# A tile's five loads each placed by its own priority on SyncE's queue, six buffers for a and v, and a new set of priorities

## The chip, the core and the metric

The kernel runs on one core of a Trainium2 chip. The metric is the device time of one execution in microseconds (us). Five engines work side by side, each through its own instructions in a fixed order: PE (matmuls and transposes on the tensor array; its weight loads are shown as PEld), DVE, ACT and POOL (elementwise work), and SP, which only issues DMA transfers. They wait for each other through semaphores.

## What is computed

A recurrent attention (RWKV-7) over 4 batches, 8 heads, 768 steps and head size 40, and then a mixer over the tokens.

```
for t in range(S):
    y[t]  = r[t] @ state
    Sa    = state @ a[t]
    state = state * w[t] - outer(Sa, b[t]) + outer(v[t], k[t])

x = y as (batch, token, 320)
theta = x @ w_theta
y2 = w_tok_r @ (x * cos(theta)) + w_tok_i @ (x * sin(theta))
u = x + y2
out = u + max(u @ w_ch, 0)
```

The time loop isn't run step by step. It is cut into chunks of 128 steps, and within a chunk it becomes matrix products.

## The kernel before

A **tile** is one chunk of 128 steps of one batch with all heads; there are 6 tiles in a batch and 24 in all, numbered 0 to 23. Each tile goes through these stages.

1. Loads (`loads`, line 414): six arrays of 160 KB in float32, `w`, `k`, `b`, `a`, `v` by SP, one transfer each, and `r` for two tiles at a time in two transfers. The tiles that take them in, `raw_w`, `raw_kb`, `raw_a`, `raw_v`, are rings of four buffers, so a load of tile i waits until tile i-4 has read its buffer.
2. `prep` (line 435): ACT takes the logarithm of `w` (`lw`, L441), PE sums it over time (`cs`, L448 to L456), ACT takes the exponential (`ex`, L460). With it `k` and `b` (`kb`, L468) and `a` (`ah`, L472) are scaled, on POOL, for the first two tiles on DVE. `v` and `r` are only cast (L477, L497). PE transposes them (L398, L505), and ACT brings the results out of PSUM (`kbT`, `aT`, `vT`, `rT`; L401, L509).
3. Scores (line 515): PE multiplies 64-row halves (L522), and DVE masks the products (L527), giving `psi`, `phi`, `lamv` and, later, `lamu`. One mask takes about 1.2 us.
4. `recurrence` (line 542): the chain from tile to tile. `x0` on PE (L555, L561) needs `psi`; ACT copies it (`nx`, L567); `nu` on PE (L573) needs `phi`; ACT copies it (L577). Then the new state `gt` (L586, L591) goes through DVE (L599), and the next tile's `x0` needs it.
5. `readout` (line 631): `lamu`, then `y` (L652, L654), and DVE writes `x` (L661). A transpose (L625) and `theta` (L670) follow.
6. The mixer, once a batch's tiles are there: sines and cosines on ACT (L690, L694), for which ACT needs another table of functions (a table load), products `zr`, `zi` on POOL (L706), rows (`row`, L724), `u` on DVE (L734), its transpose, the product with `w_ch` (L670), the sum on DVE (L743), and a store by SP (L746). The token weights are loaded by POOL (L764), transposed by PE (L772) and copied by DVE (L776).

**What sets the order.** None of these instructions is issued where it stands in the code. `add` only notes each with its engine, a cost in ns, and what it reads and writes. When all steps (their numbers run to 1456) are noted, `Plan.order` (line 95) plays the whole program through with these costs: each time it takes, for each engine, the steps that are ready, gives each a score, its priority plus `WAIT` times how much later it could start than the first that could, takes the lowest, and goes on. ACT pays `TSWITCH` in its score for a change of table. The order so found is then the order in which each engine is given its instructions. The priority is

```
o.prio = 1000.0 * (TIMES[o.spec[0]][o.spec[1]] + OFF[o.spec[2]])
```

that is, a time for the tile (or row, or weight block) plus an offset for the kind of the step. All five loads of a tile are of the kind `load`, so they have the same priority and stay in the order `w, k, b, a, v`. The numbers in `TIMES` and `OFF` were found by a search. PSUM's banks are also handed out by this play (`find`): two pairs for scores and `cs`, four single ones for the rest. Data are never read before they are there, whatever the order: each wait is a semaphore. A bad order only makes an engine wait at one instruction while others behind it could run.

Of the kernel before, what the change touches and what calls it, by code (L numbers as in the profile page):

```python
# [9 lines left out]
FP32 = mybir.dt.float32  # L10
BF16 = mybir.dt.bfloat16
AF = mybir.ActivationFunctionType
ALU = mybir.AluOpType
# [20 lines left out]
class Plan:  # L34
# [34 lines left out]
    def link(self):  # L69
        ops = self.ops  # L70
        users = {}
        for o in ops:
            o.succ = []
            o.npre = len(o.pre)
            o.start = o.end = None
            o.banks = None
            o.prio = 1000.0 * (TIMES[o.spec[0]][o.spec[1]] + OFF[o.spec[2]])
            for k in set(o.reads) | set(o.writes):
                if k[0] == "ps":
                    users.setdefault(k, set()).add(o)  # L80
        for o in ops:
            o.soft = set()
            if o.new is not None and not o.loose:
                u = users[o.new[0]]
                o.soft = {p for x in u if x is not o for p in x.pre if p not in u}
                o.soft -= set(o.pre)
            o.npre += len(o.soft)
        for o in ops:
            for p in o.pre:
                p.succ.append(o)  # L90
            for p in o.soft:
                p.succ.append(o)
        return users

    def order(self):
# [44 lines left out]
        while len(out) < n:  # L140
            pick = None
            for e, lst in ready.items():
                if not lst:
                    continue
                te = free[e]
                if e == "SP":
                    te = max(te, dma - SP_DEPTH)
                cand = []
                lo = None
                for o in lst:  # L150
                    t = max(te, est0[o])
                    b = None
                    if o.new is not None:
                        f = find(o)
                        if f is None:
                            continue
                        t = max(t, f[0])
                        b = f[1]
                    if e == "PE" and o.mode != mode:
                        t = max(t, te + (INTO64 if o.mode == 64 else OUTOF64))  # L160
                    cand.append((t, o, b))
                    if lo is None or t < lo:
                        lo = t
                if lo is None:
                    continue
                best = None
                for t, o, b in cand:
                    s = o.prio + WAIT * (t - lo)
                    if e == "ACT" and o.table is not None and o.table != table:
                        s += TSWITCH  # L170
                    if best is None or (s, o.idx) < best[0]:
                        best = ((s, o.idx), t, o, b)
                if pick is None or best[1] < pick[1]:
                    pick = best
            if pick is None:
                raise RuntimeError("no bank: " + str({e: [(o.kind, o.i) for o in l] for e, l in ready.items()}))
            _, t, o, b = pick
            ready[o.eng].remove(o)
            if o.eng == "ACT" and o.table is not None and o.table != table:
                table = o.table  # L180
                t += 1283
            o.start = t
            if o.new is not None:
                o.banks = b
                home[o.new[0]] = b
                for x in b:
                    bank_held[x] = True
            if o.eng == "PE":
                mode = o.mode
                o.end = t + o.cost + o.tail  # L190
                free["PE"] = t + o.cost
            elif o.work:
                free[o.eng] = t + o.cost
                if o.eng == "SP":
                    dma = max(dma, t + 1350.0) + o.work
                    o.end = dma + 600.0
                else:
                    s = max(t + 1800.0, dma - SP_DEPTH)
                    dma = max(dma, s) + o.work
                    o.end = min(dma, s + 2.0 * o.work) + 1000.0  # L200
            else:
                o.end = t + o.cost
                free[o.eng] = o.end - OVERLAP[o.eng]
            for k in set(o.reads) | set(o.writes):
                if k[0] == "ps":
                    left[k] -= 1
                    last_use[k] = max(last_use.get(k, 0.0), o.end + 50)
                    if left[k] == 0:
                        for x in home[k]:
                            bank_held[x] = False  # L210
                            bank_free[x] = last_use[k]
            out.append(o)
            for x in o.succ:
                x.npre -= 1
                if x.npre == 0:
                    make_ready(x)
# [10 lines left out]
def tail(n):  # L227
# [1 line left out]


OFF = dict(
    ah=-14.03, ch=37.4, cs=-41.22, ea=-6.95, egd=-90.74, egt=-28.2, ekb=21.31, enu=-16.72,
    enut=-11.56, er=-13.46, eth=-25.65, eut=-58.98, ev=17.32, ewt=-9.73, ex=39.26, exp=-63.71,
    ext=-55.21, gd=7.06, gt=16.39, kb=36.69, ln=-32.13, load=-20.04, loadr=-19.62, mlu=62.71,
    mlv=10.93, mphi=44.82, mpsi=69.12, nu=-17.14, nut=12.45, nx=-78.15, oo=13.49, r=35,
    row=38.73, sin=86.83, slu=-15.77, slv=39.92, sphi=-32.67, spsi=-35.87, st=34.23, ta=1.11,
    th=36.56, tkb=-1, tr=0.69, tv=4.86, uadd=-6.95, ut=37.54, v=-26.35, wdma=123.77, wt=37.8,
    x0=-27.08, xt=21.68, y=-40.12, z=24.68)
WAIT, TSWITCH = 435.08, 606442.0
TIMES = dict(  # L240
    tile=[
        -61.22, -38.55, -36.31, -3.78, 3.05, 10.64, 15.26, 42.47, 45.62, 46.74, 54.55, 58.02,
        77.61, 85.12, 102.64, 108.62, 104.48, 129.91, 135.62, 135.6, 150.73, 158.77, 165.34,
        174.78],
    row=[
        47.97, 37.38, 30.67, 33.44, 59.07, 74.74, 77.47, 97.12, 115.85, 115.75, 105.42, 129.53,
        141.42, 164.22, 173.87, 137.03, 124.06, 133.88, 191.51, 200.6, 184.9, 268.51, 279.77,
        212.96],
    rel=[
        -48.76, 34.55, 63.09, 65.85, -76.89, 92.41, 33.44, 33.52])  # L250


@with_exitstack
def kernel(
# [30 lines left out]
        return [consts.tile(shape, dt, name=f"{name}_{i}") for i in range(n)]  # L285

    raw_w = sb("raw_w", [128, H, D], FP32, 4)
    raw_a = sb("raw_a", [128, H, D], FP32, 4)
    raw_kb = sb("raw_kb", [128, 2, H, D], FP32, 4)
    raw_v = sb("raw_v", [128, H, D], FP32, 4)  # L290
    raw_r = sb("raw_r", [128, 2, 8 * D], FP32, 2)

    def load(i):
        bi, ci = divmod(i, NCH)
        s = i % 4

        def src(ap):
            return ap[bi, :, ci * C:(ci + 1) * C, :].rearrange("h t d -> t h d")
        return ([("raw_w", s), raw_w[s], src(w)],
                [("raw_k", s), raw_kb[s][:, 0], src(k)],  # L300
                [("raw_b", s), raw_kb[s][:, 1], src(b)],
                [("raw_a", s), raw_a[s], src(a)],
                [("raw_v", s), raw_v[s], src(v)])

    ident = consts.tile([128, 128], BF16, name="ident")
    mask_p = consts.tile([128, 1, 128], BF16, name="mask_p")
# [106 lines left out]

    def loads(i):
        for key, dst, src in load(i):
            add("SP", "load", i,
                lambda dst=dst, src=src: nc.sync.dma_start(out=dst, in_=src),
                650, [], [key], work=1030)
        bi, ci = divmod(i, NCH)
        if ci % 2 == 0:  # L420
            rr = r[bi, :, ci * C:(ci + 2) * C, :].rearrange(
                "(c g) (t q) d -> c t g (q d)", c=2, q=8)
            s = i // 2 % 2
            for c in range(2):
                add("SP", "loadr", i,
                    lambda c=c: nc.sync.dma_start(out=raw_r[s][:, c], in_=rr[c]),
                    600, [], [("raw_r", s, c)], work=520)
# [7 lines left out]
    def prep(i):  # L435
# [30 lines left out]
        for j, nm in enumerate("kb"):  # L466
# [3 lines left out]
                490 if fast else 864, [("raw_" + nm, s4), kex], [("kb", j, i % NKB)])  # L470
        add("DVE" if fast else "POOL", "ah", i,
            lambda: (nc.vector if fast else nc.gpsimd).tensor_tensor(  # L472
                out=paired(ah)[:, :, :, 0:D], in0=natural(raw_a[s4]), in1=Wi, op=ALU.mult),
            490 if fast else 864, [("raw_a", s4), kex], [("ah", i % 3)])
        copy = nc.scalar.copy if fast else nc.gpsimd.tensor_copy
        add("ACT" if fast else "POOL", "v", i,
            lambda: copy(out=paired(vb)[:, :, :, 0:D], in_=natural(raw_v[s4])),  # L477
            460, [("raw_v", s4)], [("v", i % NRV)])
        def tr(kind, kinde, srcs, dst, skeys, dkey, eng):
            p = ("ps", kind, i)  # L480
            n = 4 * len(srcs)
# [371 lines left out]
```

## Time and profile before

| | before |
|---|---|
| median of 7 runs | 216.22 us (214.56 to 216.54) |
| the profiled execution | 215.78 us |
| its span, first to last instruction | 214.0 us |
| granted clock of the tensor array | 0.996 |
| PE / DVE / ACT / POOL busy in the span | 92% / 77% / 70% / 55% |
| moved by DMA | 30.82 MB |
| share of SP's queue in the time of 16 DMA engines | 65.6% |
| median time from issue to landing, `w` / `k` / `b` / `a` / `v` | 3.9 / 4.3 / 4.0 / 4.4 / 4.3 us |
| table loads on ACT | 12, each 1.283 us |

The profile is of one execution, 0.44 us under the median. In its lists of instructions a row gives the start in us, the duration in us, the engine, the line, the operation with the tile it writes and those it reads, and how many were merged; in square brackets stands how long the engine had been idle and what ended that. In the lists of waits a row gives who waited for whom, the sum in us, how often, and the longest. Where the page shows 40 slices, a digit is the busy share of 1/40 of the span in tenths. A busy PE isn't PE at its peak, because the ends of its pipelined matmuls are modelled, so a gap of less than about 0.2 us doesn't show as idle.

### The profile page before, as it was taken

How to read it: one execution, taken by the hardware profiler on the slowest of the kernel's cores; microseconds unless marked ns; L12 is line 12 of the kernel's file. 1: busy time of each engine (PE TensorE's matmuls, PEld its weight loads, DVE VectorE, ACT ScalarE, POOL GpSimd, SP SyncE). 2: the span in 40 equal slices, each digit the busy share in tenths (PEclk: the TensorE clock that was granted, in tenths of full speed). 3: DMA queues.
4: the chain of work that ended last, by engine and by line, in shares of the span. 5: the costliest groups of instructions: out<-in, count | busy, mean ns of one | idle time of the engine just before them, and what ended most of it. 6: DMA issues, size and time to landing. Idle time of an engine off the chain costs nothing.

```text
span 214.0 us, 8107 instructions
## 1 busy us (share of the span) xinstructions
PE 196.8 (92%) x3344; PEld 157.8 (74%) x3344; DVE 165.7 (77%) x252; ACT 148.9 (70%) x340; POOL 117.5 (55%) x173
## 2 busy tenths in 40 slices
PE   1689889898999999999999999999999999999993
PEld 1467668676787777888878888887888888777771
DVE  7436797879789789869887889978979899744533
ACT  3375767799989969968787766589967996642101
POOL 5001558479666897867589225486668487050000
PEclk9999999999999999999999999999999999999998
DMA  6998989988998998974997998988986100011222
GB/s 115 228 185 164 181 171 165 226 154 145 183 174 158 181 157 157 203 127 105 223 167 173 172 186 183 187 148 194 187 192 122 35 34 3 0 34 66 88 95 92
DMA packets 134181, 30.82 MB, mean 144 GB/s; under 512 B 125824, under 2 KB 134144, under 8 KB 134144
## 3 DMA queue, kind: packets, MB, share of 16 engines
q1 hardware_dynamic: 131712, 27.54, 65.6%
q0 software_dynamic: 2432, 2.77, 8.6%
q8 instruction: 26, 0.43, 0.8%
q14 instruction: 11, 0.09, 0.1%
HBM read 29.13 MB, written 3.93 MB: 155 GB/s over the span
## 4 chain that ended last, share of the span: by engine, by line
PE 77%; ACT 7%; DVE 6%; issue 4%; DMA 2%; POOL 1%; SPq 1%; DVEq 0%; ACTq 0%; POOLq 0%
PE ps_s L724 19%; PE ps_s L398 14%; PE ps_d L522 11%; PE ps_s L670 9%; PE ps_s L625 4%; PE ps_s L573 3%; PE ps_s L505 3%; PE ps_s L591 2%; DVE phi L527 2%; DMA raw_a<-in_a_dram 2%; DVE psi L527 2%; PE ps_s L772 2%; PE ps_s L654 2%; PE ps_d L448 2%; PE ps_s L652 2%
## 5 line engine op out<-in xcount | busy, mean ns | idle before, releaser
L468 POOL TENSOR_TENSOR kb<-raw_kb,ex 128x320 bf16<-128x320 f32 x44 | 37.4, 863 | 33.7 <-ACT ex L460 32.2
L724 PE MATMUL ps_s<-zr,wtok_r 128*128 128x320 bf16 x144 | 40.7, 299 | 0.0
L724 PE MATMUL ps_s<-zi,wtok_i 128*128 128x320 bf16 x144 | 40.6, 299 | 0.0
L527 DVE TENSOR_TENSOR psi<-ps_d,mask_p 128x1024 bf16<-128x1024 f32 x24 | 29.3, 1220 | 7.3 <-PE ps_d L522 7.2
L527 DVE TENSOR_TENSOR lamu<-ps_d,mask_p 128x1024 bf16<-128x1024 f32 x24 | 29.3, 1220 | 4.7 <-PE ps_d L522 4.2
L527 DVE TENSOR_TENSOR lamv<-ps_d,mask_p 128x1024 bf16<-128x1024 f32 x24 | 29.1, 1218 | 3.0 <-PE ps_d L522 2.9
L527 DVE TENSOR_TENSOR phi<-ps_d,mask_n 128x1024 bf16<-128x1024 f32 x24 | 29.2, 1217 | 0.7 <-PE ps_d L522 0.6
L472 POOL TENSOR_TENSOR ah<-raw_a,ex 128x320 bf16<-128x320 f32 x22 | 19.0, 864 | 16.8 <-ACT ex L460 7.4
L706 POOL TENSOR_TENSOR zr<-cs,x 128x320 bf16<-128x320 f32 x23 | 17.8, 792 | 12.8 <-ACT cs L694 12.8
L460 ACT ACTIVATE ex<-ps_d 128x648 f32<-128x648 f32 x24 | 17.2, 716 | 7.7 <-PE ps_d L456 4.6
L734 DVE TENSOR_TENSOR u<-ps_s,x 128x320 bf16<-128x320 f32 x24 | 11.7, 489 | 11.2 <-PE ps_s L724 11.1
L401 ACT COPY uT<-ps_s 128x192 f32<-128x192 f32 x24 | 7.7, 321 | 17.1 <-PE ps_s L625 17.0
L706 POOL TENSOR_TENSOR zi<-cs,x 128x320 bf16<-128x320 f32 x23 | 17.8, 794 | 2.1 <-ACT cs L694 2.0
L522 PE MATMUL ps_d<-aT,kbT 64*128 64x128 bf16 x384 | 17.4, 224 | 1.1 <-DVE psi L527 0.5
L401 ACT COPY kbT<-ps_s 128x512 f32<-128x512 f32 x24 | 14.3, 594 | 4.8 <-PE ps_s L398 4.2
L724 PEld LDWEIGHTS <-wtok_r 128*128 128x128 bf16 x144 | 14.0, 97 | 4.5
L398 PE MATMUL ps_s<-ident,kb 128*128 128x128 bf16 x192 | 15.7, 227 | 1.3 <-DVE kb L468 1.3
L724 PEld LDWEIGHTS <-wtok_i 128*128 128x128 bf16 x144 | 14.1, 98 | 3.5
L522 PEld LDWEIGHTS <-kbT 64*128 64x128 bf16 x384 | 11.9, 97 | 5.2 <-issue 2.3
L743 DVE SCALAR_TENSOR_TENSOR oo<-ps_s,u 128x320 f32<-128x320 f32 x24 | 11.6, 487 | 5.2 <-PE ps_s L670 5.2
L654 PE MATMUL ps_s<-kb,lamu 128*128 128x40 bf16 x192 | 15.1, 180 | 0.4 <-DVE lamu L527 0.4
L652 PE MATMUL ps_s<-kb,lamv 128*128 128x40 bf16 x192 | 15.4, 181 | 0.0
(113 smaller groups left out, 558.9 us busy)
## 6 DMA issues: line engine op xcount, KB each, us to landing
raw_w<-in_w_dram SPq DMA_DIRECT2D x24, 160.0 KB, 3.9
raw_kb<-in_k_dram SPq DMA_DIRECT2D x24, 160.0 KB, 4.3
raw_kb<-in_b_dram SPq DMA_DIRECT2D x24, 160.0 KB, 4.0
raw_a<-in_a_dram SPq DMA_DIRECT2D x24, 160.0 KB, 4.4
raw_v<-in_v_dram SPq DMA_DIRECT2D x24, 160.0 KB, 4.3
raw_r<-in_r_dram SPq DMA_DIRECT2D x24, 160.0 KB, 3.7
out_dram<-oo SPq DMA_DIRECT2D x24, 160.0 KB, 2.3
wrow_r<-in_moe_w_tok_r_dram POOLq DMA_DIRECT2D x6, 192.0 KB, 4.9
```

The source lines that it names most:

```text
L398: nc.tensor.transpose(out=dst[:, c:c + 128], in_=pair(src, g), identity=ident)
L401: nc.scalar.copy(out=out.bitcast(FP32), in_=in_)
L460: add("ACT", "exp", i, lambda: nc.scalar.activation(out=ex, in_=ps(pk).rearrange("p a b -> p (a b)")[:, 512 - DM:512 + DM + 8], func=AF.Ex ...
L468: lambda j=j: (nc.vector if fast else nc.gpsimd).tensor_tensor(out=paired(kb[:, j])[:, :, :, 0:D], in0=natural(raw_kb[s4][:, j]), in1=invW ...
L472: lambda: (nc.vector if fast else nc.gpsimd).tensor_tensor(out=paired(ah)[:, :, :, 0:D], in0=natural(raw_a[s4]), in1=Wi, op=ALU.mult),
L522: nc.tensor.matmul(t[:, q, g, :], lhsT=lhs[rows(q), g * 128:(g + 1) * 128], rhs=rhs[rows(q), g * 128:(g + 1) * 128], start=True, stop=True)
L527: add("DVE", kindm, i, lambda: nc.vector.tensor_tensor(out=dst.rearrange("p a b c -> p (a b) c"), in0=ps(p).rearrange("p a (g c) -> p (a g ...
L652: nc.tensor.matmul(o, lhsT=lamv[:, p, g, :], rhs=kb[:, 0, h, 0:D], start=first, stop=False, skip_group_check=True)
L654: nc.tensor.matmul(o, lhsT=lamu[:, p, g, :], rhs=kb[:, 1, h, 0:D], start=False, stop=True, skip_group_check=True)
L670: nc.tensor.matmul(dst, lhsT=lhs[:, kt, :], rhs=rhs[:, kt, :], start=kt == 0, stop=kt == 2)
L706: nc.vector if fast else nc.gpsimd).tensor_tensor(
L724: nc.tensor.matmul(ps(pk)[:, 0:DM], lhsT=wtok[nm][:, s, j * 128:(j + 1) * 128], rhs=zs[c][:, s], start=n == 0 and c == 0, stop=n == NT - 1 ...
```

## The change

Each load gets a kind of its own (`lw`, `lk`, `lb`, `la`, `lv`), and so an offset of its own. Every step, moreover, gets a correction of its own by its number (`ADJ`), up to some 40 us either way. The score on PE has a new term for a change between 64-row and 128-row matmuls (`PSWITCH`, negative). `a` and `v` have rings of six buffers, not four; the other rings stay. The planner's cost of issuing a load goes from 650 to 600 ns. `OFF`, `WAIT`, `TSWITCH` and `TIMES` have new values. What is computed, and by which engine, stays.

```diff
-            o.prio = 1000.0 * (TIMES[o.spec[0]][o.spec[1]] + OFF[o.spec[2]])
+            o.prio = 1000.0 * (TIMES[o.spec[0]][o.spec[1]] + OFF[o.spec[2]] + ADJ.get(o.idx, 0.0))
...
+                    if e == "PE" and o.mode != mode:
+                        s += PSWITCH
...
-    ext=-55.21, gd=7.06, gt=16.39, kb=36.69, ln=-32.13, load=-20.04, loadr=-19.62, mlu=62.71,
...
-WAIT, TSWITCH = 435.08, 606442.0
...
+    ext=-70.75, gd=-0.66, gt=24.57, kb=0.69, la=-21.49, lb=-20.79, lk=-21.05, ln=-58.38,
+    loadr=-19.57, lv=-18.31, lw=-23.25, mlu=77.8, mlv=20.57, mphi=99.76, mpsi=106.6, nu=-4.03,
...
+WAIT, TSWITCH, PSWITCH = 398.44, 188399.0, -3357.0
...
+ADJ = {
+    0: 0.01, 1: -0.88, 2: -0.27, 3: -0.13, 4: -9.48, 5: 1.93, 6: 0.01, 7: -6.64, 8: -6.95,
...
-    raw_a = sb("raw_a", [128, H, D], FP32, 4)
+    raw_a = sb("raw_a", [128, H, D], FP32, 6)
     raw_kb = sb("raw_kb", [128, 2, H, D], FP32, 4)
-    raw_v = sb("raw_v", [128, H, D], FP32, 4)
+    raw_v = sb("raw_v", [128, H, D], FP32, 6)
...
-                [("raw_a", s), raw_a[s], src(a)],
-                [("raw_v", s), raw_v[s], src(v)])
+                [("raw_a", i % 6), raw_a[i % 6], src(a)],
+                [("raw_v", i % 6), raw_v[i % 6], src(v)])
...
-            add("SP", "load", i,
+            add("SP", "l" + key[0][4:], i,
                 lambda dst=dst, src=src: nc.sync.dma_start(out=dst, in_=src),
-                650, [], [key], work=1030)
+                600, [], [key], work=1030)
...
-                out=paired(ah)[:, :, :, 0:D], in0=natural(raw_a[s4]), in1=Wi, op=ALU.mult),
-            490 if fast else 864, [("raw_a", s4), kex], [("ah", i % 3)])
+                out=paired(ah)[:, :, :, 0:D], in0=natural(raw_a[i % 6]), in1=Wi, op=ALU.mult),
+            490 if fast else 864, [("raw_a", i % 6), kex], [("ah", i % 3)])
...
-            lambda: copy(out=paired(vb)[:, :, :, 0:D], in_=natural(raw_v[s4])),
-            460, [("raw_v", s4)], [("v", i % NRV)])
+            lambda: copy(out=paired(vb)[:, :, :, 0:D], in_=natural(raw_v[i % 6])),
+            460, [("raw_v", i % 6)], [("v", i % NRV)])
```

The first instructions on the SP queue change from `w, k, b, a, v, r, r` to `v, w, k, a, b, r, r`. On PE the transposes of tile 0's `v` come first.

## The prediction

> **What bounds the kernel now.** I read the page's shares and slices first, then busy time by stretches, then who waits for whom, then the first 24 us instruction by instruction. Busy time per engine and the 40 slices:
>
> ```profile
> PE 196.8 (92%) x3344; PEld 157.8 (74%) x3344; DVE 165.7 (77%) x252; ACT 148.9 (70%) x340; POOL 117.5 (55%) x173
> ...
> PE   1689889898999999999999999999999999999993
> ...
> DMA  6998989988998998974997998988986100011222
> ```
>
> TensorE (PE) is short of full only on the left and in the last slice. Busy time by stretches (us: PE, weight loads, DVE, ACT, POOL; clock, DMA share, GB/s) says where that ends:
>
> ```profile
> 0.00:22.00 22.00, 13.54 (x160) 10.46 (x160) 12.72 (x57) 10.91 (x23) 4.59 (x16) 1.00 1.00 174
> 22.00:40.00 18.00, 16.47 (x327) 13.59 (x328) 14.60 (x16) 13.54 (x35) 10.10 (x15) 1.00 0.97 174
> 40.00:60.00 20.00, 17.56 (x362) 13.91 (x360) 17.24 (x20) 18.18 (x40) 15.85 (x22) 1.00 0.94 176
> 60.00:76.00 16.00, 15.21 (x306) 12.42 (x305) 13.57 (x18) 14.45 (x31) 11.62 (x18) 1.00 0.94 169
> 76.00:90.00 14.00, 13.51 (x235) 10.87 (x233) 12.66 (x16) 11.88 (x25) 12.55 (x19) 1.00 0.99 171
> 90.00:210.00 120.00, 119.81 (x1962) 96.27 (x1961) 93.98 (x129) 80.00 (x189) 62.76 (x87) 1.00 0.60 123
> ```
>
> From 90 to 210 us PE never waits. So time can only be won before 90 us, or by giving PE less to do.
>
> How much less? The timeline shows a warm 128-column transpose every 0.055 us, a 64-row score matmul every 0.026, a 320-column one every 0.136, an 80-column one every 0.036, a 40-column one at the floor of 0.025. Times their counts (872, 768, 496, 320, and 768 with 120 tiny ones) this is 48.7 + 20.0 + 67.4 + 11.5 + 22.2 = 169.7 us. The array also changes between 64-row and 128-row matmuls 130 times; the median surplus in the timeline is 0.097 us going in and 0.122 coming out, 14.2 us in all. So 183.9 of the 214.0 us is work, 30.1 us is lost. I place the loss by two events: `nu` of tile 1 and the first row of the mixer.
>
> ```profile
> 12.06 0.45 PE L573 MATMUL ps_s<-nx,phi 128*128 128x40 bf16 x8 [0.68 <-DVE phi L527]
> ...
> 23.88 0.37 PE L573 MATMUL ps_s<-nx,phi 128*128 128x40 bf16 x8
> ```
>
> By 23.88 us PE has done 8.4 us of work (its groups before that one, at the prices above): 15.5 us lost, part of it the slow clock of the start. The first row starts at 75.72 us with 52.6 done: 7.6 us lost in the middle. From there to the end 7.0 are lost, 3.3 of them after the last matmul. In the middle tiles follow each other every 6.2 us (`nu` of tile 1 at 23.88, of tile 9 at 73.35) while PE needs 41.9/8 = 5.2 us for one; the SP queue issues a tile's loads every 5.7 us (`w` of tile 1 at 6.09, of tile 10 at 57.61). What PE waits for between 22 and 90 us:
>
> ```profile
> PE ps_s L398 <- ACT nu L577: 0.9, 3, 0.4
> PE ps_s L555 <- ACT gd L609: 0.6, 1, 0.6
> PE ps_d L522 <- DVE phi L527: 0.6, 1, 0.6
> PE ps_s L561 <- ACT lw L441: 0.5, 1, 0.5
> ```
>
> Many short waits for ACT and DVE, none for a load: the order decides here, not the DMA, though DMA is at 0.94 to 1.00.
>
> **What the Trainium skill says.** "TensorE: Matmul & The Clock Gate", section "Back-to-back issue gap", gives N/2.4 + 2.5 ns per warm matmul, N/1.2 cold; the trace agrees (0.055 us at 128 columns warm; 0.40 us for four at 17.44 us, cold). Its section on the clock gate wants about 3.4 us of sustained work to warm; here PE is slow until some 22 us. "DMA: Bandwidth & Descriptors", section "Issuing engines are not separate DMA queues", says all queues share the same 16 engines; so six buffers and another order on SP add no bandwidth, and the DMA share near 1.0 agrees. "Trainium Kernel Development and Optimization", under best practices, warns that matmul busy time is no measure of distance from the roofline; hence the count of work above.
>
> **The change part by part**, read off the order of the instructions in both built programs.
>
> Same work: all matmuls, masks and bytes are kept. Mode changes go from 130 to 128: 2 x 0.11 = -0.2 us. Two more activation-table loads (14 against 12), 2 x 1.283 us on ACT: the added pair stands between the sines of the sixth and of the seventh half-batch, late, where PE is always busy and ACT holds 80 of 120 us; the cover is ACT's 40 idle us, price nothing, at worst +2.6. The planner's new `PSWITCH` is worth 3357/398 = 8 ns of waiting, nothing. The tail is the same: six row matmuls, the last `u` transposes, the last `wch` products, two stores.
>
> Head, by hand. SP issues at 0.73, 1.24, 1.85, 2.73, 3.41 us; I keep these places and give them to `v, w, k, a, b`. The landings of before by place: 3.69 (ACT starts), about 4.7 and 5.4 (3.2 to 3.8 after issue), 7.28 (chain), 7.9 (3.9 to 4.7 after).
>
> ```profile
> 0.73 0.44 SPq L417 DMA_DIRECT2D raw_w<-in_w_dram  x1
> 1.24 0.57 SPq L417 DMA_DIRECT2D raw_kb<-in_k_dram  x1
> 1.85 0.84 SPq L417 DMA_DIRECT2D raw_kb<-in_b_dram  x1
> 2.73 0.63 SPq L417 DMA_DIRECT2D raw_a<-in_a_dram  x1
> ```
>
> So `lw` starts at 4.75, 1.06 late; `cs` +0.5, `ex` +0.85 and 0.71 long: 6.8. `kb(k)` to 7.3, `ah` to 7.8, `kb(b)` 7.9 to 8.4, its transposes and `kbT` (1.07 + 0.59) to 10.1, scores 10.15, `phi` and `psi` (now in this order) 10.85 to 13.2, `x0` 13.25, `nx` 0.48 later for 0.43, `nu` of tile 0 at 14.2: 2.1 us later than 12.06. But tile 1 is no longer queued behind it: the transposes of `r` and `cs` of tile 1 now stand before `x0` on PE, so `ex` of tile 1 ends at 13.35 (14.94 before), and its `kb(k)` and `ah` stand on DVE ahead of `lamv` and `gt`. `nu` to ACT 15.1, `gt` 16.5, `kb(b)` of tile 1 16.9, `kbT` 18.6, its scores 18.7 (20.47 before), `phi`, `psi` to 21.75, `nu` of tile 1 at 22.6. That is -1.3 us, with an error of some 0.7 either way. By then PE has done 9.5 us of work, 1.1 more than before; since PE does not bind the middle, I count 0.3 of it. Head: -1.6 us (bounds -2.9 and +2.1).
>
> Middle. The two orders are alike: `nu` of tile 9 after 50.7 us of work (50.3), the first row after 50.9 (52.6). What differs is the distance on PE between a group and the one that needs it. Between the scores of `phi` and `nu` stood 1.1 to 2.6 us of other PE work for tiles 1 to 5, now 2.8 to 5.5: waits for `phi` go. `psi` now follows `phi`, so `x0` gains little. Other distances shrink: `nu` to its transpose and `gt` to its own become tighter in several tiles. Adding up, over ten tiles, by how much each distance falls short of its latency in the trace (0.7 to 1.45 us, with 2.4 for the second of a pair of masks) I get some 10 us before and 14 after; these overlap, so it is a warning and not a sum. Bounds: -3.6 (all waits but 4.0 us of the 7.6 gone) and +3.5. I take -1.0, the `phi` waits at PE and its weight loads in this stretch (0.6 + 0.3 + 0.7, not all on the path).
>
> Six buffers for `a` and `v`: SP waits for its buffers in the middle, but those transfers land well before use; no PE wait there names a load. Price nothing; if the middle speeds up, they keep the loads ahead, at most the step from 6.2 to 5.7 us a tile. On SP the loads are moved past each other and past stores, which wait for `oo` on DVE: SP waited 48.5 us in all for that before. The first store stands at place 80 of SP's queue, before at 87; behind it are the loads of tile 13 and later, needed some 100 us into the run, and a late one costs first its lead. On POOL the weight loads keep their places but for swaps within a pair. Nothing for both, at worst +1.
>
> Last stretch: PE has 13.6 us left after the last `theta`, not 19.7. The path from there through two sines (0.48 each) and two products (0.49 each) to the last row chunks is some 2.5 us; other rows cover it. Price nothing.
>
> Sum: -0.2 - 1.6 - 1.0 = -2.8 us. The profiled execution took 215.78 us (214.0 and 1.78 around it), so 213.0; the median shown is 216.22, 0.44 above it, so **213.4 us**.
>
> **The rivals.** Bigger gain: the middle runs at the pace of the loads, 8 x 0.5 = -4.0 instead of -1.0, 210.4. For it: buffers and phi distances; against it: DVE and ACT are at 0.86 and 0.91 from 40 to 60 us. Nothing: the middle's pace is set by DVE, ACT and DMA together, and what the head wins waits there: 216.0. For it: the same shares, and equal order. Slower: `v` in front costs tile 0 2.1 us and tile 1 does not make it up, because its `kb(b)` on DVE stands behind `gt` of tile 0, at the end of the late chain: 216.22 + 2.1 = 218.3. It decides if scores of tile 1 start after 20.47 us. That the change doesn't do what it says (six buffers that free nothing) is inside the forecast, which takes nothing from them.
>
> **How the numbers follow.** Forecast 0.48, bigger gain 0.14, nothing 0.18, slower 0.20. About 0.5% (1.1 us) is what a measurement of this kernel tells from no change. Faster: 0.48 + 0.14 = 0.62; same 0.17; slower 0.21 (the slower case and a little of "nothing"). The range of 210.4 to 217.6 holds the bigger gain at its edge, nothing, and the mild part of slower.
>
> **What would show it.** Right: first matmul earlier (the `v` transposes), `nu` of tile 0 near 14, of tile 1 before 23.9, first row before 75, PE still full from 90 us, DMA shares as before. Wrong: scores of tile 1 after 20.5; PE idle between 22 and 76 above the 4.8 us of now; PE waits for loads; idle after 90 us.

## The result, and the profile after

| | before | after |
|---|---|---|
| median | 215.99 us (31 runs, 214.56 to 216.78) | 214.53 us (12 runs, 213.49 to 215.06) |
| profiled execution, its span | 215.78, 214.0 us | 214.94, 213.2 us |
| first row of the mixer | 75.72 us | 73.02 us |

The changed kernel takes 0.9932 of the time before (95% interval 0.9913 to 0.9950): 1.5 us less. In this document medians and ratios leave out the executions in a slow state (lower granted clock, longer time), which only e4 (two of six) and e5 (three of 18) had. All line numbers after are those of before plus 201; in the experiments they shift again. The page's busy times and slices:

```profile
PE 197.7 (93%) x3344; PEld 157.1 (74%) x3344; DVE 165.8 (78%) x252; ACT 152.3 (71%) x342; POOL 117.4 (55%) x173
...
PE   1579989999989999999999999999999999999993
...
DMA  6989989999999889995999899889897000002122
```

The shape is the old one: holes on the left, full from 90 us on. Busy time by stretches, columns as before:

```profile
0.00:22.00 22.00, 13.53 (x163) 10.77 (x163) 13.42 (x58) 11.30 (x23) 4.97 (x16) 1.00 0.89 159
22.00:40.00 18.00, 17.17 (x346) 14.24 (x344) 15.10 (x17) 13.98 (x36) 10.54 (x16) 1.00 1.02 177
40.00:60.00 20.00, 18.24 (x360) 14.56 (x355) 17.06 (x19) 17.98 (x41) 16.75 (x24) 1.00 1.04 183
...
90.00:210.00 120.00, 119.69 (x1939) 93.92 (x1935) 93.08 (x128) 83.16 (x192) 63.17 (x88) 1.00 0.60 122
```

PE is busier from 22 to 60 us (35.41 us against 34.03), and in its waits between 22 and 90 us no long one is left:

```profile
PE ps_s L774 <- ACT nx L768: 0.6, 2, 0.4
PE ps_d L649 <- DVE phi L728: 0.4, 1, 0.4
PE ps_s L599 <- ACT nu L778: 0.3, 1, 0.3
PE ps_d L723 <- ACT ex L661: 0.3, 1, 0.3
PE ps_d L723 <- DVE phi L728: 0.3, 1, 0.3
PE ps_d L649 <- ACT lw L642: 0.2, 1, 0.2
```

These rows sum to 2.1 us; the ten of before came to 4.9. That looks like the forecast's middle coming true. The head, first ACT and then PE in the list of instructions, looks worse than forecast:

```profile
11.82 0.47 ACT L642 ACTIVATE lw<-raw_w 128x320 bf16<-128x320 f32 x1 [1.66 <-DMA raw_w<-in_w_dram]
```

```profile
12.35 0.43 PE L649 MATMUL ps_d<-lw,ntri_inc 128*128 128x320 bf16 x1 [0.75 <-ACT lw L642]
...
13.02 0.43 PE L762 MATMUL ps_s<-v,psi 128*128 128x40 bf16 x8
...
14.27 0.43 PE L774 MATMUL ps_s<-nx,phi 128*128 128x40 bf16 x8 [0.28 <-ACT nx L768]
...
20.13 0.83 PE L723 MATMUL ps_d<-aT,kbT 64*128 64x128 bf16 x16
...
24.18 0.36 PE L774 MATMUL ps_s<-nx,phi 128*128 128x40 bf16 x8
```

`lw` of tile 1 waits 1.66 us for its load, `cs` of tile 1 (12.35) waits for `lw`, and `x0` of tile 0 (13.02) is queued behind `cs`. The scores of tile 1 start at 20.13 us (forecast 18.7; before 20.47) and its `nu` at 24.18 (forecast 22.6; before 23.88). Read alone, this trace says: nothing won in the head, something in the middle. The experiments show the reverse.

### The profile page after: what moved, and what is told of

Its sections match the earlier page's. It is cut to its first block, busy times and chain, and to the rows that moved or that the text cites. A ratio compares the mean times of both kernels' runs of the same rounds, so it can differ in the third digit from the quotient of the medians.

```text
span 213.2 us, 8059 instructions
## 1 busy us (share of the span) xinstructions
PE 197.7 (93%) x3344; PEld 157.1 (74%) x3344; DVE 165.8 (78%) x252; ACT 152.3 (71%) x342; POOL 117.4 (55%) x173
## 4 chain that ended last, share of the span: by engine, by line
PE 70%; DVE 5%; ACT 3%; issue 2%; ACTq 0%; DVEq 0%
PE ps_s L925 19%; PE ps_s L599 11%; PE ps_d L723 9%; PE ps_s L871 8%; PE ps_s L826 4%; DVE phi L728 2%; PE ps_s L792 2%; PE ps_s L973 2%; PE ps_s L706 2%; PE ps_s L774 2%; PE ps_s L855 2%; PE ps_s L853 1%; PE ps_s L846 1%; PE ps_s L762 1%; PE ps_d L649 1%
## 5 line engine op out<-in xcount | busy, mean ns | idle before, releaser
L673 POOL TENSOR_TENSOR ah<-raw_a,ex 128x320 bf16<-128x320 f32 x22 | 19.0, 864 | 30.6 <-issue 18.7
L602 ACT COPY uT<-ps_s 128x192 f32<-128x192 f32 x24 | 7.5, 318 | 15.5 <-PE ps_s L826 14.2
L862 DVE TENSOR_TENSOR x<-ps_s,ex 128x320 bf16<-128x320 f32 x24 | 11.7, 486 | 8.2 <-PE ps_s L855 4.1
L723 PE MATMUL ps_d<-aT,kbT 64*128 64x128 bf16 x384 | 16.8, 223 | 0.8 <-ACT kbT L602 0.7
L944 DVE SCALAR_TENSOR_TENSOR oo<-ps_s,u 128x320 f32<-128x320 f32 x24 | 11.6, 488 | 5.2 <-PE ps_s L871 4.5
```

Of the source, the lines that this page charges most:

```text
L602: nc.scalar.copy(out=out.bitcast(FP32), in_=in_)
L673: lambda: (nc.vector if fast else nc.gpsimd).tensor_tensor(out=paired(ah)[:, :, :, 0:D], in0=natural(raw_a[i % 6]), in1=Wi, op=ALU.mult),
L723: nc.tensor.matmul(t[:, q, g, :], lhsT=lhs[rows(q), g * 128:(g + 1) * 128], rhs=rhs[rows(q), g * 128:(g + 1) * 128], start=True, stop=True)
```

## The experiments

In most of them the order found by the planner is written out as a list of step numbers for each engine, `SEQ`, so that one stretch can be exchanged and the rest stays:

```diff
+                lst = [o for o in lst if o.idx == SEQ[e][done[e]]]
                 te = free[e]
```

Ratios are to runs of the kernel before on the same chip, whose medians were 215.7 to 215.8 us.

### Head and rest exchanged

e1: every step of before's plan up to `nu` of tile 1 in the old order, all later steps in the new one. e2: the other way round.

```diff
-SEQ = after
+SEQ = [before, up to nu of tile 1] + [the rest, in the order of after]     # e1
+SEQ = [after, up to nu of tile 1] + [the rest, in the order of before]     # e2
```

> The changed kernel, its order written out as lists, with every step up to nu of tile 1 in the order of the kernel before (loads w, k, b, a, v first) and all later steps in the new order. If the head is what was won, about -0.8 to -1.3 us are given back: some 215.4 us, nu of tile 1 near 23.9 us, the stretch after it as in the changed kernel. If the middle swallows what the head wins (rival: nothing to be had in the head), it stays at about 214.5. If the head matters more than thought, it is as slow as before, 216.0.

> The other way round: every step up to nu of tile 1 in the new order (v, w, k, a, b), all later steps in the order of the kernel before. If head and rest add up, this gives what the head alone is worth: about 215.0 (-1.0 us). If the head's gain needs the new middle to be kept, 216.0. If the head is all, 214.5.

Measured: e1 215.86 us, ratio 1.0016 (0.9995 to 1.0036); e2 214.41 us, 0.9936 (0.9910 to 0.9963). The new head alone gives the whole gain, the new rest gives nothing.

The new rest with the new head (the changed kernel, 0.9932) is no faster than the old rest with it (e2). How the head pays is seen in `nu` of tiles 3 and 9, PE's list, first before, then e2:

```profile
37.51 0.36 PE L573 MATMUL ps_s<-nx,phi 128*128 128x40 bf16 x8
73.35 0.35 PE L573 MATMUL ps_s<-nx,phi 128*128 128x40 bf16 x8
```

```profile
36.22 0.36 PE L870 MATMUL ps_s<-nx,phi 128*128 128x40 bf16 x8
72.06 0.35 PE L870 MATMUL ps_s<-nx,phi 128*128 128x40 bf16 x8
```

Both are 1.29 us earlier, and so is the first row (75.72 to 74.43): from tile 3 to the first row the program is shifted, rigidly; at the last matmul 1.0 of it is left (210.65 to 209.64). Yet `nu` of tile 1 was only 0.33 us earlier in e2 (23.55). What differs besides is the work that PE has behind it there, 9.5 us against 8.4. If that work counts in full, the shift should be 0.33 + 1.1, about 1.4 us; it is 1.29. The other pair, e1 and the changed kernel, has the new rest: there the new head brings `nu` of tile 1 0.37 us later (24.18, in e1 23.81), the count gives 1.1 - 0.37, about 0.7, and `nu` of tile 9 comes 0.91 earlier (72.82, in e1 73.73). So the sum of time and work done ahead fits both shifts within 0.2 us. Which of the steps moved ahead bring it was not tried one by one.

`nu` of tile 1 itself hardly tells the heads apart: it was at 23.88, 23.81 and 24.04 with the old one (before, e1, e3) and at 24.18, 23.55, 23.90 and 23.31 with the new one (after, e2, e4, e5; the last two load tile 1 as `w, k, b, a, v`), means 23.91 and 23.74.

### Six buffers alone

e3: six buffers for `a` and `v` as in the change, every engine in before's order.

```diff
-SEQ = after
+SEQ = before
```

> Six buffers for a and v and the load's cost, but every engine's order that of the kernel before. My step: nothing, 216.0 within 0.5 us, although SP's waits for buffers of a and v fall. Rival (the loads' pace sets the middle): up to -2 us, 214.

Measured: 215.48 us, 0.9995 (0.9976 to 1.0014). In the old order the buffers bring nothing. The new order with four buffers was not tried, so whether it needs the six stays open.

### The loads' own places

e4: the changed kernel with SP's whole queue in before's order but for its first seven loads. e5: only the loads permuted, `w, k, b, a, v` tile by tile, in the places of the queue that hold loads in the changed kernel; stores and `r` stay.

```diff
-SP: lv0 lw0 lk0 la0 lb0 r r lw1 lk1 la1 lb1 lv1 lw2 lb2 lk2 la2 r r lv2 ... stores, loads
+SP: lv0 lw0 lk0 la0 lb0 r r lw1 lk1 lb1 la1 lv1 lw2 lk2 lb2 la2 lv2 r r ... both as in before    # e4
+SP: lv0 lw0 lk0 la0 lb0 r r lw1 lk1 lb1 la1 lv1 lw2 lk2 lb2 la2 r r lv2 ... stores as in after   # e5
```

> The changed kernel with the loads of tile 1 and later grouped w, k, b, a, v a tile on SP, at the places they had before; tile 0's five, and all other engines, in the new order. No PE wait named a load between 22 and 90 us, so by my theory it stays at 214.5 within 0.5 us. Rival: the placing of each load is what lets the new order run; then 215.5 or more, with waits for DMA at POOL and PE.

> The changed kernel with the loads of tile 1 and later again grouped as w, k, b, a, v, but now put into the very places of SP's queue that hold loads in the changed kernel, so that no load changes its side of a store by grouping a whole queue. If the slow-down of the first grouped kernel came from a load standing behind a store that waits for its sum, it is gone: 214.5 within 0.7 us. If each load's own place is what counts, it stays above 217.

Measured: e4 220.48 us, 1.0233 (1.0189 to 1.0278); e5 216.39 us, 1.0044 (1.0021 to 1.0068). Both slower than the changed kernel, and up to the first row equal to it or ahead (72.97 and 72.32 us). e4's profiled execution is its longest, 223.58 us at a mean clock of 0.974; the four that the median counts have 0.992. It shows where the time goes, but not how much of the 220.48 us. In the stretch from 130 to 150 us:

```profile
130.00:150.00 20.00, 15.25 (x215) 11.73 (x214) 10.06 (x13) 9.62 (x22) 8.73 (x13) 0.74 0.82 163
```

Who SP waited for between 120 and 140 us, and POOL's list there:

```profile
SPq L1043 <- DVE oo L1040: 4.7, 1, 4.7
```

```profile
140.88 0.45 POOL L774 CAST v<-raw_v 128x320 bf16<-128x320 f32 x1 [6.04 <-DMA raw_v<-in_v_dram]
```

A store stands in SP's queue and waits 4.7 us for its sum. Behind it are all loads of tile 18, which before's order puts behind those of tile 19, the new order ahead of them. POOL takes tile 18 first in the new order: it stands 6.04 us at the cast of that tile's `v`, with its `r`, `ah` and `kb` queued behind. PE is idle for 4.75 of 20 us, and on top its clock is at 0.74 there, a dip of which the shorter executions, by their mean clock, have less. In e5, without the store in the way, PE has one wait after 90 us,

```profile
PE ps_s L802 <- POOL r L794: 1.6, 1, 1.6
```

for the `r` of tile 18, behind the same cast of `v` (it waited 2.7 us here, for a load now last of its tile and behind tile 19). In e2 the same grouped loads cost nothing, with before's order on the other engines. So the loads' order has to agree with the order of the engines that take them in; by itself neither wins. In both kernels the swap of tiles 18 and 19 came with the grouping, so what the placing inside a tile is worth by itself stays open.

### v in front

e6: before with `v` of tile 0 first on SP, ACT (`v`, then `lw`) and PE. e7: the changed kernel with it moved back.

```diff
-SP: lw lk lb la lv      ACT: ln exp ekb ea v ev      PE: cs tkb ta spsi sphi tv
+SP: lv lw lk lb la      ACT: v ln ev exp ekb ea      PE: tv cs tkb ta spsi sphi     # e6, tile 0
...
-SP: lv lw lk la lb      ACT: v ln ev exp ea ekb      PE: tv cs ta tkb sphi spsi
+SP: lw lk la lb lv      ACT: ln exp ea ekb v ev      PE: cs ta tkb sphi spsi tv     # e7, tile 0
```

> The kernel before with one thing of the new head: v of tile 0 is loaded, cast and transposed first (v, w, k, b, a), all the rest in the order of before. By my step v in front costs: lw 0.7 to 1.1 us later, nu of tile 0 near 13, and the end some 0.5 to 1 us later, 216.5. Rival, v in front is what wins the head: 214.5 to 215.0.

> The changed kernel with v of tile 0 taken from the front to the fifth place (w, k, a, b, v), its cast and transposes after those of a and b. By my theory the head wins by what stands in front of x0 on PE and in front of gt on DVE, not by v: nu of tile 0 comes at 13.3 to 13.7 us instead of 14.27, and the time is 214.0 to 214.5. Rival: v in front is needed; then tile 0 is later than 14.27 and the time 215 or more.

Measured: e6 216.20 us, 1.0026 (1.0013 to 1.0039); `nu` of tile 0 at 13.61 us (12.06), of tile 1 at 24.77, of tile 9 at 74.23 (73.35): again a rigid shift, +0.88. e7 214.87 us, 0.9965 (0.9950 to 0.9981): no faster than the changed kernel. The scores of tile 0 start earlier, 8.68 instead of 9.60, but its `nu` comes at 14.31, because `x0` still stands behind `cs` of tile 1. In the old head `v` in front costs 0.6 us; in the new one moving it back wins nothing.

### A faster head by hand

e8: both tiles' first loads ahead of `r`, `cs` of tile 1 right behind `x0` of tile 0, its `kb` and `ah` ahead of `gt`, its scores ahead of `r`, `lamv` and `lamu`. e9: e7 with `w` of tile 1 ahead of `v` and `r` on SP, and `x0` ahead of the transposes of `r` on PE.

```diff
-SP: lv0 lw0 lk0 la0 lb0 r r lw1 lk1 la1 lb1 lv1
-PE: tv0 cs0 ta0 tkb0 sphi0 spsi0 tr0 cs1 x00 slv0 nu0 ta1 nut0 gt0 slu0 gd0 tv1 tkb1 cs2 y0 sphi1
+SP: lw0 lk0 lb0 la0 lv0 lw1 lk1 lb1 la1 r r lv1                                                    # e8
+PE: cs0 tkb0 ta0 spsi0 sphi0 tv0 x00 cs1 nu0 nut0 gt0 tkb1 ta1 gd0 spsi1 sphi1 tr0 slv0 tv1 slu0 x01 nu1 cs2 y0
+SP: lw0 lk0 la0 lb0 lw1 lv0 r r lk1 la1 lb1 lv1                                                    # e9
+PE: cs0 ta0 tkb0 sphi0 spsi0 tv0 cs1 x00 tr0 slv0 nu0 ta1 nut0 gt0 slu0 gd0 tv1 tkb1 cs2 y0 sphi1
```

> A head written by hand, the rest as in the changed kernel: loads w, k, b, a, v of tile 0, then w, k, b, a of tile 1 ahead of r, psi ahead of phi, cs of tile 1 right behind x0 of tile 0, its kb and ah ahead of gt and its scores ahead of the transposes of r and of lamv and lamu. If what counts is how early tile 1 gets through (with all later tiles moved by as much), its scores start at 15.5 to 17.5 us instead of 20.13, nu of tile 1 near 20 to 21.5 and the time is 212 to 213. Rival: the loads set the pace after the head, so that tiles 2 to 9 come no earlier; then 214 to 214.5.

> The changed kernel with v of tile 0 behind (as in the w-first run), w of tile 1 loaded ahead of v and r, and x0 of tile 0 ahead of the transposes of r, still behind cs of tile 1. If the new head is held up by lw of tile 1 waiting for its load (1.66 us in the changed kernel) with x0 of tile 0 queued behind it on PE, nu of tile 0 comes at 13 us or earlier instead of 14.27, all later tiles come 0.7 to 1.3 us earlier, and the time is 213.3 to 213.8. If tile 1 is bound elsewhere (its mask or its kb), tiles 2 to 9 stay where they are and it is 214.5.

Measured: e8 218.76 us, 1.0138 (1.0111 to 1.0165); e9 215.74 us, 0.9995 (0.9982 to 1.0007). Both missed, by the same kind of mistake. PE's list in e8:

```profile
15.38 1.04 PE L819 MATMUL ps_d<-aT,kbT 64*128 64x128 bf16 x16
...
21.58 0.42 PE L745 MATMUL ps_d<-lw,ntri_inc 128*128 128x320 bf16 x1
...
25.97 1.03 PE L695 MATMUL ps_s<-ident,kb 128*128 128x128 bf16 x8
...
28.21 0.69 PE L819 MATMUL ps_d<-aT,kbT 64*128 64x128 bf16 x16
```

The scores of tile 1 come 4.75 us earlier, as meant (15.38), and `nu` of tile 1 at 21.21. But `cs` of tile 2 had been left behind it (21.58; in the changed kernel 18.79), and POOL's products and the scores of tile 2 hang on it: 28.21 instead of 24.47. Besides, eight transposes still take 1.03 us at 25.97; the changed kernel has 0.62 at 22.49. In e9 ACT's order was changed in one place only, `lw` of tile 1 ahead of the cast of `r`; `rT` stayed ahead of `nx`:

```profile
13.22 0.59 ACT L806 COPY rT<-ps_s 128x512 bf16<-128x512 bf16 x1 [1.50 <-PE ps_s L802]
13.70 0.72 ACT L757 ACTIVATE ex<-ps_d 128x648 f32<-128x648 f32 x1
14.30 0.43 ACT L864 CAST nx<-ps_s 128x320 bf16<-128x320 f32 x1
```

`nx` of tile 0 stands behind `rT` on ACT, which waits for the transposes of `r` that the edit had put behind `x0`. `nu` of tile 0 came at 14.79 us, later than without the edit. So e9 doesn't tell what an early `w` of tile 1 is worth.

### The slow array

e10 and e11: matmuls of zeros into a free PSUM bank, 30 before everything, in e11 22 more in holes of the head.

```diff
+    warm_up(30)                                                # e10 and e11
     for o in order:
...
         o.fn()
+        warm_up(MORE.get((o.kind, o.i), 0))                    # e11
+MORE = {("cs", 0): 14, ("tkb", 0): 5, ("spsi", 0): 3}
```

> The changed kernel with 30 matmuls of zeros, 128 columns each, ahead of everything on PE (from about 0.9 us to 4.1, where PE did nothing), into a PSUM bank that is free. What is computed stays. In the changed kernel a 128-column transpose takes 0.102 to 0.107 us up to 18 us and 0.05 after; in the fast head, whose PE work had more holes, until 28 us. If that slow array is a part of what the head loses, the matmuls up to some 12 us go at 0.055 us, nu of tile 1 comes 1 to 2.5 us earlier, later tiles as much, and the time is 212 to 213.5. If the array falls back into the slow clock in the holes of the head, or the masks and casts are the chain, 214.5.

> The same with 14 more such matmuls after cs of tile 0, 5 after its transposes of kb and 3 after its scores, in holes of PE. If 3 us of work at the start aren't enough to get and keep the fast clock, these do it: 212 to 213 us. If the start is enough, they cost a little where they stand in the way: 0.2 to 0.5 us over the run with 30 alone.

Measured: e10 213.78 us, 0.9903 (0.9881 to 0.9925); e11 213.35 us, 0.9888 (0.9863 to 0.9913), from 4 and 5 runs. These are the fastest two, ahead of the changed kernel's 0.9932 with intervals that overlap or touch. PE's list in e11:

```profile
0.99 3.38 PE L1025 MATMUL ps_s<-warm 128*128 128x128 bf16 x30 [0.99 <-DVE off_diag L523]
...
7.52 0.40 PE L604 MATMUL ps_s<-ident,ah 128*128 128x128 bf16 x4 [0.62 <-DVE ah L678]
...
13.22 0.61 PE L604 MATMUL ps_s<-ident,ah 128*128 128x128 bf16 x4
...
22.06 0.36 PE L779 MATMUL ps_s<-nx,phi 128*128 128x40 bf16 x8
...
109.56 0.51 PE L978 MATMUL ps_s<-ident,wrow_r 128*128 128x128 bf16 x6 [0.80 <-DMA wrow_r<-in_moe_w_tok_r_dram]
```

Four transposes take 0.40 us at 7.52, 0.61 again at 13.22. `nu` of tile 1 is at 22.06, of tile 9 at 70.69 (72.82 in the changed kernel) and the first row at 70.89 (73.02): 2.13 us earlier. At the end 1.1 are left, mostly because PE now waits 0.80 us for a load of token weights.

But not all of the 2.13 us is the clock. In e11 `lw` of tile 1 found its load 1.39 us earlier than in the changed kernel (11.82), with the same order on SP:

```profile
10.43 0.47 ACT L647 ACTIVATE lw<-raw_w 128x320 bf16<-128x320 f32 x1 [0.82 <-DMA raw_w<-in_w_dram]
```

From the start of this `lw` to `nu` of tile 1 the changed kernel, e2, e4, e5 and e7 take 12.3 to 12.6 us, e11 11.6 us. So in this profile some 0.7 to 1.0 us is the faster array, and the rest an earlier load, which the matmuls of zeros aren't shown to cause. In e10 the array was slow until 16.6 us all the same, and `lw` of tile 1 happened to find its load (10.37 us, no wait), so how much of e10's gain is the clock stays open.

e12: 19 more such matmuls, and the token-weight transposes that had waited moved behind `gt` of tile 13.

```diff
-MORE = {("cs", 0): 14, ("tkb", 0): 5, ("spsi", 0): 3}
+MORE = {("cs", 0): 14, ("tkb", 0): 5, ("spsi", 0): 3, ("tr", 0): 8, ("cs", 1): 8, ("slv", 0): 3}
-PE: nu13 ch4 ch3 wt12 wt12 th12 tr14 nut13 gt13 tv14
+PE: nu13 ch4 ch3 th12 tr14 nut13 gt13 wt12 wt12 tv14
```

> Two things put together on the changed kernel. First the matmuls of zeros as in the run with more of them, with 8 further ones after the transposes of r, 8 after cs of tile 1 and 3 after lamv's scores, where the array had fallen back to the slow clock (0.61 us for four transposes from 13.2 to 16.8 us). Second, the last token-weight transposes stand behind gt of tile 13 on PE instead of ahead of theta of tile 12, because PE had now come early enough to wait 0.80 us for their load. If both hold, nu of tile 1 comes at 21.2 to 21.8 us (22.06), no wait for wrow is left, and the time is 212.0 to 212.9. If the gain of the start is lost later in another way, it stays at 213.3.

Measured: 214.83 us, 0.9956 (0.9936 to 0.9976), slower than e11. The array was now fast from about 6 us on, but `lw` of tile 1 waited for its load until 11.23 us, and `nu` of tile 1 came at 22.30: there the load is the bound (from `lw` to `nu` it is 11.1 us, less than in e11). And the move made a new wait, on DVE:

```profile
111.57 0.56 DVE L1078 COPY wtok_r<-ps_s 128x768 bf16<-128x768 bf16 x1 [1.94 <-PE ps_s L1074]
112.04 0.55 DVE L1078 COPY wtok_i<-ps_s 128x768 bf16<-128x768 bf16 x1
112.50 1.22 DVE L829 TENSOR_TENSOR psi<-ps_d,mask_p 128x1024 bf16<-128x1024 f32 x1
```

The copies of the moved transposes kept their place, and `psi` behind them came late; PE waited 1.1 us for it.

## Why the prediction was right

- **The total.** Forecast 213.4 us, measured 214.53, in the range and faster, as forecast. Of -2.8 us about half came; what is missing is mainly the middle's 1.0.
- **Head, -1.6.** The size held (e2: 0.64% of 215.7 is 1.4 us), its two terms did not; that it held is luck, because two errors cancelled. The first: "`nu` of tile 1 at 22.6, -1.3" was 24.18, later than before, and 23.55, -0.3, in e2. Step by step in the changed kernel: `ex` of tile 1 ended at 13.90 us and not 13.35, because `lw` waited for its load (0.55). The transposes of `v` of tile 1 stood on PE ahead of those of `kb`, so `kbT` ended at 19.61 and not 18.6 (0.46 more). `y` of tile 0 (19.50 to 20.13) stood ahead of the scores, which so came at 20.13 and not 18.7 (0.42 more); the last 0.15 comes after them.

```profile
17.51 0.63 PE L599 MATMUL ps_s<-ident,v 128*128 128x128 bf16 x4
17.94 1.06 PE L599 MATMUL ps_s<-ident,kb 128*128 128x128 bf16 x8
19.50 0.19 PE L853 MATMUL ps_s<-kb,lamv 128*128 128x40 bf16 x1
```

  The late load isn't the main part: in e2 `ex` ended at 13.39, as forecast, and `nu` of tile 1 still came 0.95 us late. The second error: "Since PE does not bind the middle, I count 0.3" of the 1.1 us done in advance. It counts in full, within 0.2 us, as the two pairs of heads show.
- **Middle, -1.0.** Nothing (e1: 0.16% slower than before, interval -0.05 to 0.36%). The named waits went, from 4.9 to 2.1 us, but by the count of work the loss between `nu` of tile 1 and the first row stayed: 7.6 us before, 7.4 after (73.02 - 24.18, less 50.9 - 9.5 us of work). The waits of PE between 22 and 90 us don't even go with the time: they sum to 4.6 us in e2, which has the whole gain, and to 2.6 us in e1, which has none. A short wait removed at one instruction came back as smaller gaps, or as work that ran ahead and waited elsewhere; which, the runs don't tell. The forecast had read a list of waits as a sum to be won.
- **`v` in front, +2.1 for tile 0.** 14.27 against the forecast 14.2, but by another path: the forecast let `x0` wait for `psi`, which was done at 12.68; `cs` of tile 1 in front of `x0` sets it. So in the new head it isn't the price of `v` (e7).
- **Six buffers, nothing.** Right in the old order (e3).
- **SP's and POOL's moves, nothing, at worst +1.** Right as a price of the change. The reason given, that a late load costs first its lead, doesn't hold in general: e5 only permutes loads and costs 1.1% (1.0044 against 0.9932).
- **Table loads, nothing.** Consistent: after, with 14, and e2, with 12, take 0.9932 and 0.9936; not tried apart.
- **The last stretch.** From the first row to the end 7.4 us are lost, before 7.0. The 0.4 wasn't looked for.
- **The slower rival** was to decide if the scores of tile 1 came after 20.47 us. They came at 20.13, and the rival's reason, that tile 1 doesn't make up for tile 0, was nearly so; what saved the forecast was the work done ahead.

## What to carry to other kernels

When only the start of a program changes, compare two kernels at the same event by its time and by the work already done before it; here the sum of the two differences is what moved the later tiles, within 0.2 us, even where PE isn't full. It holds only while the next tile isn't held up: in e8 `nu` of tile 1 came 2.97 us earlier than in the changed kernel with 2.9 us less work done, which would leave the end where it was, and `nu` of tile 9 came 3.88 us later, because `cs` of tile 2 was late. A list of PE's waits isn't what their removal would win. Who moves a step on one engine must move its partners on the others and look at the next tile too: e8, e9 and e12 each lost by a step that was left where it stood.

## What the runs showed of the hardware

- The array's slow clock lasted until some 20 us in the changed kernel (an 8-transpose group took 1.06 us at 17.94, 0.62 at 22.49) and until 28 us in e8. In e11 it ended at about 6 us and was back from 13.2 to some 16.5 us. The column of the granted clock shows 1.00 through the slow start of all these kernels, where only the durations tell; the fall back in e11 it does show, in the third slice of the page and as a mean of 0.57 from 13 to 17 us, 0.50 from 14 to 16 us:

```profile
PEclk9979999999999999999999999999999999999999
```

  The Trainium skill, "TensorE: Matmul & The Clock Gate", part 1 on the HAM clock gate, speaks of one busy window of about 3.4 us, free-running: 30 matmuls in 3.38 us, which need not fill such a window, were not enough in e10, where the array stayed slow until 16.6 us. With the clock at a half, a mean of 0.57 over 4 us makes the fall back in e11 some 3.4 us long, about one such window.
- The landing of one and the same load varies: `lw` of tile 1, with its `w` at the same place of SP's queue, started at 11.82 us in the changed kernel, at 10.43 in e11, at 10.37 without a wait in e10, at 11.23 in e12; the load was issued at 6.07, 5.89, 5.75 and 5.67 us. With `nu` of tile 1 at 23.31 to 24.18 us under one head, a single profile can't tell 0.5 us there.
